# One attention and mixing kernel: x of batches 4 and 5 and the residual of batch 3 transposed by DMA instead of TensorE, in a new order of all steps

## The chip, the cores and the metric

The kernel runs on one core of a Trainium2 chip. The metric is device time in microseconds (us), the median of several executions. A NeuronCore has five engines that run side by side: TensorE (PE in the profile, with its weight loads as PEld), VectorE (DVE), ScalarE (ACT), GpSimd (POOL) and SyncE (SP), which here only issues DMA transfers. They wait for each other through semaphores. TensorE writes to PSUM, eight banks of 2 KB for each of 128 partitions; VectorE and ScalarE bring results from there to SBUF.

## The reference

```python
# attention: q, k, v are (8, 8, 576, 64)
q_d = q.reshape(B, H, Sd, 4, D).mean(axis=3)        # the same for k and v
out_up = np.repeat(sm_attn(q_d, k_d, v_d), 4, axis=2)
mask = np.abs(pos[:, None] - pos[None, :]) < 4
out_local = softmax(where(mask, scale * q @ k.T, -1e9)) @ v
x = (out_up + out_local).transpose(0, 2, 1, 3).reshape(B, S, H * D)   # (8, 576, 512)
# mixing
theta = x @ w_theta
zr, zi = x * cos(theta), x * sin(theta)
u = x + einsum('ts,bsd->btd', w_tok_r, zr) + einsum('ts,bsd->btd', w_tok_i, zi)
return u + np.maximum(u @ w_ch, 0.0)
```

Inputs and output are float32; the kernel works in bfloat16 inside and sums in float32.

## The kernel before

All eight batches go through the same chain of small steps, and several batches are under way at once. Each step has a two-letter name, and one step is one to a few dozen instructions of one engine:

- `lk`, `lq`, `lv`, `lw` load k, q and the two halves of v into one of 14 staging buffers (tile `st`), `ck`, `cq`, `cv` cast them. `tp` transposes k or q on TensorE (L304), `ev` brings the result to SBUF (L317). For batch 7 the DMA transposes them instead (`dk`, L308), from the cast to a staging buffer.
- The coarse attention takes means of four (`kd`, `qd`, L323 on VectorE or L331 with L334 and L337 on GpSimd), `sd`, `ed`, `nd`, `xn` (L427 to L459). The local attention is computed in windows of 64 positions: scores `ps` (L483, in 64*64 tiles), exponential `ex` (L491, ScalarE), product with a band mask `mk` (L502, VectorE or GpSimd), product with v `po` (L512), division `nm` (L520 and L521, VectorE).
- `xt` (L531) transposes the local output, `xa` (L537) adds the coarse one: the tile `xT` holds x with the channels on the partitions, in four column blocks of 128 channels.
- `th` (L548) multiplies x by w_theta, `cs` takes cosine and sine (L553, L554). z needs x with the positions on the partitions. `xm` (L587) transposes x on TensorE into PSUM, four 128x128 matmuls for 128 positions, and `zz` (L594, VectorE) multiplies it by cosine and sine. For the batches in `XDMA` there is no `xm`: `dx` (L590) has the DMA transpose one block of 128 channels for 512 positions from `xT` into the tile `xx`, four for a batch, and `zz` reads `xx`. The last 64 positions go their own way (`tt`, `ct`, `zt` L569, and `zp` on TensorE or `dz` L573 by DMA).
- `mx` (L610) is the mixing product over positions, nine matmuls for 288 columns; `ua` (L615) adds x and gives `uT`. `ch` (L635) multiplies by w_ch, and `rl` (L640) adds the residual and stores into `osb`. The residual is u with positions on the partitions, tile `ur`: for batches in `RPE` transposed on TensorE (`up`, L624) and copied (`uc`, L627), for the others by DMA (`du`, L619), four transfers for a batch. `st` (L644) stores.

There is one `xx`; of `xT`, `uT`, `ur` and `z` there are two each, taken in turn by batches. What engine runs a step, and into which bank pair or staging buffer, stands in the words of a long string `ORDER`; a word such as `x12` is a step's name and its place. Each engine runs its instructions in the order of that string, and nothing else sets it. Words with `wm` are matmuls on a constant tile that only keep TensorE active while it would wait (L715).

```python
XDMA = (6, 7)
RPE = (0, 1, 2, 3)
    def zz(b, c, w):
        x = xx[:, c, :] if b in XDMA else at.pop(("xm", b, c))
        nc.vector.tensor_tensor(out=z[b % 2][:, 2 * c:2 * c + 2, :],
                                in0=x.unsqueeze(1).to_broadcast([P, 2, DM]),
                                in1=cs[(4 * b + c) % NCS], op=ALU.mult)
```

Of the kernel before, what the change touches and what calls it, by code (L numbers as in the profile page):

```python
# [42 lines left out]

NSTG = 14

XDMA = (6, 7)

RPE = (0, 1, 2, 3)
ZPE = (0, 1, 2, 3)

QKD = (7,)
# [7 lines left out]
cqg lq7 lk8 lk9 tp45 cqg kcg kcg x12 lqa eva lqb kdg cvv kca cka wm62 tp67 lkc x13 lkd cvv eva ckv wm13 pv01 cqv lq0  # L59
la2 cqg lb1 tp45 qdv eva wm22 tp23 eva wm65 ps67 kdg vdv lq3 qdv ckg cka ps45 cag ex wm25 sd23 ex lb4 ed cbg lk5 sd01  # L60
cqg ps67 mkv ed po45 nm po23 nd45 nd01 la6 nm la7 xn xn lk8 mkg tp23 cag po45 ex xt6 po01 cqa eva la9 lqa mkg caa xd7
lqb ckg xca ckg nm tp23 nm xt4 xt5 lbd cag lbc cbg lb2 xt7 xa cqg lb1 eva lb0 cbg lb3 lb6 tp01 xa po23 th4 xa xm5 xa
lv7 cqg nm cbg th6 lw xt7 cbg th2 lv5 xm3 evv cbg ts cs tp01 lv8 lv9 cs cbg xa tt4 zz cs xm5 wp6 wp2 zz lw lw wp3 lw
lv4 lw cbg lqa zz ct lqd eva qdg ztv wp7 cba th4 wcv zp5 lkb xm6 wcv lkc kdg wcv wp2 wp3 wcv zcv wp0 wcv wp1 cs wp7
wca wcv ps45 lk2 lk1 wcv wcv ps23 te ex qdg ps01 lq0 zz kdv cva ex mx7 mx6 mx4 cvg ua sd23 cvg cvg mkv lc3 ex po01 ua
sd67 ed ed mkv mx5 ua nm po23 ua po01 cvg pv67 nm nm mkg vda mx4 ua po23 lq6 cqg po67 nd01 nm nd45 mx2 up3 xn lq7 ckg
xn cqg lk5 cka nm tp01 xd4 lk8 up5 uca eva xcv xt3 ucv lk9 tp67 cka xt4 xt0 ua ckg xt1 kdg lv4 xa xa xa mx5 xa eva lva
tp23 ua th4 xt0 lw xa evv cqg th5 xm1 lvb lcd lqc tt0 lw lk1 lv2 lv0 lw ts cs lw xm4 cqg cs tp67 ckg cqg th2 xm3 th5
ct lw cka zz tp01 cs qdg zz cs xm2 evv ztg lc6 lc5 zp4 mx6 ccg zz qdg zcv zz eva cvg mx7 ps45 te ex ua ps23 ua ckg kdv
ex mkv ps01 mx6 lq7 mx7 po45 sd23 ex lq8 lk3 kdg ed cvg sd01 cqg ckg ua lk4 lq9 mx6 tp23 mkv lva lw lvc lw nm ua tp45  # L70
up7 cvg mkv cvv ed mx0 eva cvg pv23 ccg ua ucv eva po67 po45 ua nm up1 nm vda ccg ccg ch0 nd67 lq1 xn nd23 lkb cqg cqa
tp45 uca qdg xn mx1 xd2 xt3 eva ps67 rl lq0 ua po45 xcv kdg qdg ps01 ch2 xa ckg ex mkg nm rl mx3 ps67 cqg lv2 cka po45
ex ua sd01 lkd xt2 ckg ex nm mx3 xt4 xt5 xa up2 ua cqa cqg tp67 cvv ed up3 xa evv uca th0 xa lv6 xt1 up2 xa lw th4 xm6
ucv ts cs uca th5 cvg lq5 ckg po01 cvg zz cs nm po23 xm7 cs ch6 nm tt4 tp01 lw ct tp23 th5 rl mkg ch4 lq7 zz st eva
evv rl po67 sd01 cs cqg cvg ztg po23 ch5 nm nm rl ch4 lv8 lw te ed cvg st pv67 vda zp0 zca lk4 cka lk3 lk1 tp23 cqa
mkg ckg lq9 lqb rl qdg lva lw xm1 eva ckg utg lv0 zz lw xm5 ch4 nd67 lvc zz xn lw nd01 mx5 lvd xn mx6 st ps23 rl lv2
ua po01 kdg nm ps45 ua mx7 lk5 ex xd0 cqa xt1 ex up6 ua xcv ucv lk6 kdv tp23 cqg utg mx0 tp45 qdg xa ua eva sd67 xt2
lv8 xt3 ch1 eva xa mkg ed xa th0 mkv rl cvg lk3 lw xt6 xt7 xa xa lw lk1 cvg th2 mx1 ua ts cs xm3 cvg tt0 zz th6 st lq4
cs cvg cka po45 dt cvg ckg ct po23 th7 mx1 ztg lk7 cs lvb nm pv45 cs ckg po67 cqg kdg lw nm ua sd23 mx0 cvg nm te ed
zp1 tp67 vdv zcv ht2 tp45 xm1 rt lw ua lq9 mx3 eva zz ps67 eva ua lva qdg po45 nm ex ps01 lq0 ex xm2 up3 zz lqc nd67  # L80
uca lvd tp45 cqa xm2 qdg xn nd01 zz mx3 cka cka xn mx2 xd0 up1 lk2 lv6 kdg st ua mx3 cqa mkv lw uca xcv eva tp67 xt0
up1 lk5 ua ua cva ucv xt4 xa mx5 st xa st eva ps23 mkg sd01 qdg po67 lw ed ua nm lv3 xt4 mx5 xt6 cva mx7 po01 ua ex
sd23 xa xa po45 lw nm cvg th6 nm lq4 cqv xt0 lw ed cvv xa ts cs tp23 mkv lv8 th1 cs xm4 ua ch5 kdg lw rl ch6 lv9 eva
tt0 th1 th7 xm5 pv23 utv ct ztg zz up0 ss cqg cs zz vdv mx1 uca ua xm0 lv1 lw st zz cs tp45 lv7 cvg lv0 cvg lqb nd23
# [17 lines left out]
def kernel(  # L102
# [53 lines left out]
    rl = tiles(2, [P, 2, 4], "rl", FP32)  # L156
# [509 lines left out]
    def span(*ns):  # L666
# [3 lines left out]
        return out  # L670

    STEPS = dict(
        k0=(lambda i, w: None, span(1)), kc=(kc, span(4)), la=(la, span(4)), ca=(ca, span(4)), lb=(lb, span(9)), cb=(cb, span(9)), lc=(lc, span(4)), cc=(cc, span(4)),
        wp=(wp, [(j,) for j in WPJ]), wc=(wc, [(j,) for j in WPJ]),
        lk=(load(0), span(B, 4)), lq=(load(1), span(B, 4)), ck=(cast(0), span(B, 4)), cq=(cast(1), span(B, 4)),
        tp=(tp, [x for x in span(B, 2, 2) if x[0] not in QKD]), dk=(dk, [x for x in span(B, 2, 2) if x[0] in QKD]), ev=(ev, span(B, 2, 2)),
# [48 lines left out]
    for kind in todo:  # L725
        assert next(todo[kind], None) is None, kind
    assert set(x[0] for x in at) <= {"v", "ot"}, at


# [28 lines left out]
```

## Time and profile before

| | |
|---|---|
| median of 3 runs | 230.73 us (230.29 to 231.62) |
| span of the profiled execution | 229.4 us; its own time was not taken apart from the runs, and the median lies 1.3 us above its span |
| PE busy | 219.7 us (96%), 3491 matmuls |
| DVE, ACT, POOL busy | 185.6, 159.3, 144.1 us |
| DMA queue of SP | 83.4% of 16 engines over the span |

The span runs from the first to the last instruction. Busy time counts the instructions of an engine; a busy PE may still be a PE that is filled with short or badly packed matmuls. Group rows read: line, engine, operation, written tile, read tiles, count, then busy us and mean ns of one. Rows of a timeline begin with start and length in us; a bracket at the end holds the idle time before and who ended it. Rows of a stretch hold its bounds and length, the busy time of PE, PEld, DVE, ACT and POOL with instruction counts, TensorE's granted clock, DMA share and GB/s. Rows of a tile give shortest, median and longest duration in ns.

### The profile page before, as it was taken

To read this page: it belongs to the slowest core of one execution; us is meant where nothing else is said; L and a number is where in the kernel's file an instruction comes from. 1 tells how busy PE (TensorE), PEld (TensorE's weight loads), DVE (VectorE), ACT (ScalarE), POOL (GpSimd) and SP (SyncE) were. 2 spreads that over 40 slices of the span, in tenths; PEclk is the share of its full clock that TensorE was granted. 3 is DMA by queue.
4 is the path that set the end of the run, shared out by engine and by line. 5 is a ranking of instruction groups with operands and counts; after the bars stand their busy time and mean duration, and the time that the engine had idled before them with its cause. 6 is when DMAs were issued, how large, how long until landed. Compare 5 with 4: busy or idle time off the path is not lost.

```text
span 229.4 us, 8506 instructions
## 1 busy us (share of the span) xinstructions
PE 219.7 (96%) x3491; PEld 154.2 (67%) x3491; DVE 185.6 (81%) x377; ACT 159.3 (69%) x239; POOL 144.1 (63%) x190
## 2 busy tenths in 40 slices
PE   7898899999999999999999999899999999999992
PEld 2455778696778765776788667676676665677740
DVE  5168999999899899797898969979898889476382
ACT  2389899759987899689887896779879258600000
POOL 7768999929999989991984456892697310200000
PEclk9999999999999999999999999999999999999998
DMA  6999999999989999999998007996576357376677
GB/s 181 387 391 391 268 190 222 374 271 226 235 270 249 248 345 177 231 261 233 291 220 211 21 17 191 302 214 126 136 132 187 68 118 206 74 207 160 94 239 241
DMA packets 76647, 49.35 MB, mean 215 GB/s; under 512 B 61120, under 2 KB 61120, under 8 KB 76608
## 3 DMA queue, kind: packets, MB, share of 16 engines
q1 hardware_dynamic: 76608, 48.81, 83.4%
q8 instruction: 27, 0.44, 0.8%
q14 instruction: 12, 0.10, 0.1%
HBM read 33.98 MB, written 9.44 MB: 189 GB/s over the span
## 4 chain that ended last, share of the span: by engine, by line
PE 86%; DVE 7%; DMA 3%; issue 2%; SPq 1%; ACT 0%; POOL 0%; DVEq 0%
PE PS L610 30%; PE PS L548 12%; PE PS L635 12%; PE PS L304 5%; PE PS L531 4%; PE PS L512 3%; DMA st<-in_v_dram 3%; PE PS L587 2%; PE PS L483 2%; PE PS L448 2%; PE PS L560 2%; DVE tmp L521 2%; PE PS L624 2%; PE PS L652 2%; PE PS L453 1%
## 5 line engine op out<-in xcount | busy, mean ns | idle before, releaser
L610 PE MATMUL PS<-WT,z 128*128 128x288 bf16 x576 | 77.9, 286 | 0.2 <-issue 0.2
L610 PEld LDWEIGHTS <-z 128*128 128x128 bf16 x576 | 54.3, 98 | 15.8 <-issue 0.9
L615 DVE TENSOR_TENSOR uT<-PS,xT 128x288 bf16<-128x288 f32 x64 | 28.8, 452 | 11.8 <-PE PS L610 10.9
L548 PE MATMUL PS<-wth,xT 128*128 128x512 bf16 x128 | 32.2, 379 | 0.0
L635 PE MATMUL PS<-wch,uT 128*128 128x512 bf16 x128 | 31.1, 379 | 0.0
L569 POOL TENSOR_TENSOR zT<-xT,cst 128x512 bf16<-128x512 bf16 x7 | 8.1, 1153 | 34.0 <-ACT cst L566 34.0
L521 DVE TENSOR_TENSOR tmp<-PS,rl 128x512 bf16<-128x512 f32 x40 | 27.7, 692 | 1.4
L502 POOL TENSOR_TENSOR pm<-pm,band 128x1024 bf16<-128x1024 bf16 (+1 forms) x14 | 25.0, 1789 | 4.5 <-ACT pm L491 4.5
L537 DVE TENSOR_TENSOR xT<-PS,xdT 128x464 bf16<-128x464 f32 (+1 forms) x40 | 24.0, 629 | 3.0 <-ACT xdT L471 2.0
L640 DVE SCALAR_TENSOR_TENSOR osb<-PS,ur 128x512 f32<-128x512 f32 x32 | 21.8, 685 | 4.7 <-PE PS L635 4.2
L491 ACT ACTIVATE pm<-PS 128x1024 bf16<-128x1024 f32 (+1 forms) x24 | 20.4, 879 | 6.5 <-PE PS L483 6.5
L553 ACT ACTIVATE cs<-PS,pihc 128x512 bf16<-128x512 f32 x32 | 22.2, 693 | 1.6 <-PE PS L548 1.4
L720 ACT ACT_TABLE_LOAD x15 | 19.2, 1283 | 0.3
L331 POOL TENSOR_TENSOR two<-kT 128x580 f32<-128x580 bf16 x13 | 15.0, 1152 | 7.0 <-ACT kT L317 5.3
L635 PEld LDWEIGHTS <-uT 128*128 128x128 bf16 x128 | 11.9, 98 | 11.1
L554 ACT ACTIVATE cs<-PS 128x512 bf16<-128x512 f32 x32 | 19.2, 601 | 0.0
L594 DVE TENSOR_TENSOR z<-PS,cs 128x1024 bf16<-128x1024 bf16 x24 | 16.0, 682 | 2.3 <-PE PS L587 1.8
L548 PEld LDWEIGHTS <-xT 128*128 128x128 bf16 x128 | 11.3, 98 | 9.6 <-DVE xT L537 0.2
L331 POOL TENSOR_TENSOR two<-qT 128x576 f32<-128x576 bf16 x13 | 14.9, 1145 | 4.3 <-ACT qT L317 4.0
L438 ACT ACTIVATE pd<-PS 128x864 bf16<-128x864 f32 x16 | 13.8, 888 | 5.0 <-PE PS L427 4.9
L397 POOL CAST v_w<-st 128x512 bf16<-128x512 f32 x26 | 16.8, 672 | 0.0
L317 ACT COPY qT<-PS 128x1152 bf16<-128x1152 bf16 x13 | 14.6, 1121 | 2.0 <-PE PS L304 2.0
(116 smaller groups left out, 427.0 us busy)
## 6 DMA issues: line engine op xcount, KB each, us to landing
st<-in_k_dram SPq DMA_DIRECT2D x32, 288.0 KB, 6.0
st<-in_q_dram SPq DMA_DIRECT2D x32, 288.0 KB, 6.1
st<-in_v_dram SPq DMA_DIRECT2D x70, 128.0 KB, 5.2
out_dram<-osb SPq DMA_DIRECT2D x32, 256.0 KB, 2.4
st<-in_v_dram SPq DMA_DIRECT2D x4, 288.0 KB, 3.2
st<-in_moe_w_tok_r_dram SPq DMA_DIRECT2D x4, 288.0 KB, 6.5
st<-in_moe_w_tok_i_dram SPq DMA_DIRECT2D x4, 288.0 KB, 7.4
st<-in_moe_w_theta_dram SPq DMA_DIRECT2D x4, 256.0 KB, 6.3
```

The costliest lines, as they stand in the source:

```text
L331: nc.gpsimd.tensor_tensor(out=t, in0=src[:, :, 0:2], in1=src[:, :, 2:4], op=ALU.add)
L491: nc.scalar.activation(out=pm[(3 * b + u) % NPM][:, :, 0:n].rearrange("p e c j w -> p e (c j w)"), in_=at.pop(("ps", b, u))[:, :, 0:4 * W ...
L502: EW[w].tensor_tensor(out=t, in0=t, in1=m, op=ALU.mult)
L521: nc.vector.tensor_tensor(out=tmp[(NCH * b + c) % NTMP].rearrange("p g (j d) -> p g j d", d=D), in0=ps[:, :, :, 0:D], in1=r.unsqueeze(3).t ...
L537: nc.vector.tensor_tensor(out=xT[b % 2][:, :, CH * c:CH * c + cnt].rearrange("p e (m j) -> p e m j", j=4), in0=at.pop(("xt", b, c))[:, :, ...
L548: nc.tensor.matmul(out=ps, lhsT=xT[b % 2][:, dc, P * c:P * c + P], rhs=wth[:, dc, :], start=(dc == 0), stop=(dc == 3))
L553: nc.scalar.activation(out=t[:, 0, :], in_=ps, func=AF.Sin, bias=pihc, scale=1.0)
L554: nc.scalar.activation(out=t[:, 1, :], in_=ps, func=AF.Sin, bias=0.0, scale=1.0)
L610: nc.tensor.matmul(out=ps, lhsT=z[b % 2][:, j, P * dc:P * dc + P], rhs=WT[:, j, cols], start=(j == 0), stop=(j == 8))
L615: nc.vector.tensor_tensor(out=uT[b % 2][:, dc, cols], in0=at.pop(("mx", b, i)), in1=xT[b % 2][:, dc, cols], op=ALU.add)
L635: nc.tensor.matmul(out=ps, lhsT=uT[b % 2][:, dc, P * c:P * c + P], rhs=wch[:, dc, :], start=(dc == 0), stop=(dc == 3))
L640: nc.vector.scalar_tensor_tensor(out=o, in0=at.pop(("ch", b, c)), scalar=0.0, in1=ur[b % 2][:, c, :], op0=ALU.max, op1=ALU.add)
```

## The change

Two lists of batches change, so that x of batches 4 and 5 and the residual of batch 3 go through `dx` and `du` instead of `xm` and `up`. `ORDER` is replaced as a whole. The batches' steps need no longer come in rising order: a word now carries the step's indices (`tp011.01` is batch 0, pair 1, q, into banks 0 and 1). Line numbers after L46 move by 32: L590 becomes L622, L610 L642, and so on.

```diff
-XDMA = (6, 7)
-
-RPE = (0, 1, 2, 3)
+XDMA = (4, 5, 6, 7)
+
+RPE = (0, 1, 2)
...
 ORDER = """
-l10 l11 c1g c1g k0 l12 lk3 l14 ckg c1v lk5 wm0b t101 c1g e1a kcg wm24 t123 e1a lq6 wm45 x12 cva ckg x13 cva x10 cvv
...
+l103.0 lq02.1 cq02.a lq03.2 c103.a cq03.v l100.3 c100.g l101.4 wm.28 tp011.01 ev011.v qd01.v l102.5 c101.g wm.24
...
-    todo = {kind: iter(seq) for kind, (_, seq) in STEPS.items()}
+    todo = {(kind,) + tuple(args) for kind, (_, seq) in STEPS.items() for args in seq}
     for word in ORDER.split():
-        kind, place = word[:2], word[2:]
+        word, _, place = word.partition(".")
+        kind, args = word[:2], tuple(int(x) for x in word[2:])
...
-        STEPS[kind][0](*next(todo[kind]), place)
+        todo.remove((kind,) + args)
+        STEPS[kind][0](*args, place)
```

The order moves on every engine. Two places, before and now:

SyncE's queue where batch 5's x is under way. Before, it holds the transposes of batch 7's k and q (L308), of batch 4's residual (L619), of a tail (L647) and of batch 5's rest of z (L573), loads of v (L349) and stores (L644):

```order
L308 DMA_TRANSPOSE st_135<-k_tm_76 128x9x128
L644 DMA out_dram<-osb_121 128x512
L308 DMA_TRANSPOSE st_138<-q_tm_79 128x9x128
L647 DMA_TRANSPOSE utr<-ut_117 128x4x128
L619 DMA_TRANSPOSE ur_114<-uT_112 128x4x128
L349 DMA st_132<-in_v_dram 64x8x64
L619 DMA_TRANSPOSE ur_114<-uT_112 128x4x128
L308 DMA_TRANSPOSE st_129<-k_tm_74 128x9x128
L349 DMA st_128<-in_v_dram 64x8x64
L308 DMA_TRANSPOSE st_136<-q_tm_77 128x9x128
L573 DMA_TRANSPOSE z_104<-zT 128x4x128
```

Now, with x of batch 5 (L622), k and q of batch 7 (L340), loads of q (L320), a store (L676) and the rest of z (L605):

```order
L622 DMA_TRANSPOSE xx<-xT_102 128x4x128
L320 DMA st_132<-in_q_dram 128x576
L622 DMA_TRANSPOSE xx<-xT_102 128x4x128 x2
L340 DMA_TRANSPOSE st_133<-k_tm_74 128x9x128
L676 DMA out_dram<-osb_123 128x512
L320 DMA st_134<-in_q_dram 128x576
L340 DMA_TRANSPOSE st_140<-k_tm_76 128x9x128
L605 DMA_TRANSPOSE z_104<-zT 128x4x128
L622 DMA_TRANSPOSE xx<-xT_102 128x4x128
```

The four transfers of x come in, two transposes and the rest of z stand between the third and the fourth of them, and the residual of batch 4 is later in the queue.

VectorE where batch 4's z is made. Before, z (L594) takes x from PSUM (PS) and cosine and sine from `cs`; with copies for the coarse attention (L413, L416), L615 and L640 in between:

```order
L594 TENSOR_TENSOR z0_103<-PS_61,cs0_105 128x1024
L594 TENSOR_TENSOR z0_103<-PS_61,cs1_106 128x1024
L413 CAST vd1_73<-PS_61 128x8x64
L416 CAST vd1_73<-PS_61 32x4x64 x2
L615 TENSOR_TENSOR uT1_113<-PS_61,xT1_102 128x288
L594 TENSOR_TENSOR z0_103<-PS_61,cs2_107 128x1024
L640 SCALAR_TENSOR_TENSOR osb0_119<-PS_61,ur0_114 128x512
```

Now (L626 is z, L647 was L615, L552 and L553 were L520 and L521, L672 was L640):

```order
L626 TENSOR_TENSOR z0_103<-xx_110,cs1_106 128x1024
L647 TENSOR_TENSOR uT1_113<-PS_61,xT1_102 128x288
L552 RECIPROCAL rl0_93<-PS_61 128x8
L553 TENSOR_TENSOR tmp1_88<-PS_61,rl0_93 128x512
L626 TENSOR_TENSOR z0_103<-xx_110,cs0_105 128x1024
L672 SCALAR_TENSOR_TENSOR osb2_121<-PS_61,ur0_114 128x512
L626 TENSOR_TENSOR z0_103<-xx_110,cs2_107 128x1024
L626 TENSOR_TENSOR z0_103<-xx_110,cs3_108 128x1024
```

z reads `xx`, which is in SBUF, and its four instructions stand in the order 1, 0, 2, 3 of positions.

More of the change, by code (lines that the diff above doesn't have):

```diff
@@ L63 @@
[L63 to L72, printed above, removed]
@@ L98 @@
+ch72.7 rl72.v ch71.1 rl71.v st72 st71
 """
@@ L722 @@
             continue
-        STEPS[kind][0](*next(todo[kind]), place)
+        todo.remove((kind,) + args)
+        STEPS[kind][0](*args, place)
         pin()
-    for kind in todo:
-        assert next(todo[kind], None) is None, kind
+    assert not todo, todo
     assert set(x[0] for x in at) <= {"v", "ot"}, at
```

101 lines of the change are left out of this document (71 added, 30 removed).

## The prediction

> **What bounds the kernel now.** I read the page first: shares of the engines, then the chain that ended last.
>
> ```profile
> span 229.4 us, 8506 instructions
> PE 219.7 (96%) x3491; PEld 154.2 (67%) x3491; DVE 185.6 (81%) x377; ACT 159.3 (69%) x239; POOL 144.1 (63%) x190
> PE 86%; DVE 7%; DMA 3%; issue 2%; SPq 1%; ACT 0%; POOL 0%; DVEq 0%
> ```
>
> TensorE (PE) is busy for 96% and carries 86% of the chain. A busy PE is not a PE at its peak, so next come the stretches: busy time after 28.8 us, when the first product of x and w_theta (L548) starts.
>
> ```profile
> 28.80:160.00 131.20, 130.03 (x2346) 95.82 (x2343) 116.42 (x230) 110.90 (x168) 102.29 (x124) 1.00 0.93 223
> 125.00:160.00 35.00, 34.06 (x571) 23.84 (x562) 29.14 (x61) 28.22 (x42) 22.52 (x25) 1.00 0.68 146
> ```
>
> PE is busy 130.03 of 131.20 us to 160 us, so 1.17 us are lost there. VectorE (DVE) is second with 116.42 us, which is 89%. DMA is 0.68 busy between 125 and 160 us. So the time is the sum of PE's steps, each at its start-to-start distance, plus a start that PE spends waiting and a tail. PE's timeline gives the distances.
>
> ```profile
> 102.58 1.03 PE L548 MATMUL PS<-wth,xT 128*128 128x512 bf16 x4
> 103.45 0.57 PE L531 MATMUL PS<-ident,tmp 128*128 128x116 bf16 x8
> ...
> 106.51 1.03 PE L548 MATMUL PS<-wth,xT 128*128 128x512 bf16 x4
> 107.47 0.45 PE L512 MATMUL PS<-v_w,pm 64*64 64x65 bf16 x32
> ...
> 114.01 0.39 PE L587 MATMUL PS<-ident,xT 128*128 128x128 bf16 x4
> 114.23 1.02 PE L610 MATMUL PS<-WT,z 128*128 128x288 bf16 x7
> ```
>
> The first column is a step's start. Four transposes of x (L587) take 114.23 - 114.01 = 0.22 us; four of a residual (L624) are the same instruction on the same shape. A product of four L548 takes 0.87 us when a full-array step follows (102.58 to 103.45) and 0.96 us when one in 64*64 tiles does (106.51 to 107.47): going over to small tiles costs 0.09 us.
>
> **The change part by part.** *Transposes that leave PE.* x of batches 4 and 5 is 8 steps, the residual of batch 3 is 4: 12 x 0.22 = 2.6 us, all on the path, since PE has no idle time that could swallow it. The eight x steps lose no VectorE work: the product z (L594) is made either way, and costs the same (below). The four residual copies (L627) go from ScalarE and VectorE, off the path.
>
> *Tile shapes.* Counted step by step in the two orders, changes of the array's tile shape rise from 101 to 109. But those between full rows and 128*72 cost nothing in the trace; those into or out of 64*64, 128*32 and 128*64 are 76 before and 70 after. 6 x 0.09 = 0.5 us gained. In the count of all changes, the new order does not do what its words say. The bank pairs were neighbours before too, except that one score step now takes banks 3 and 4: nothing.
>
> *What the transfers cost.* Twelve DMA transposes come on the SyncE queue. The rows of the tile xx show what such a one costs for batches 6 and 7.
>
> ```profile
> L590 SPq DMA_TRANSPOSE xx<-xT x8: 1189/1264/2213, 179.1 to 199.6; - x8
> L594 DVE TENSOR_TENSOR z<-xx,cs x8: 682/682/692, 191.7 to 206.5; 128x1024 bf16<-128x1024 bf16 x8
> DMA to landing us min/median/max: 2.4/2.5/3.3
> L308 SPq DMA_TRANSPOSE st<-k_tm x2: 1318/1819/2320, 147.0 to 158.1; - x2
> ```
>
> Each holds the queue for 1.26 us and lands 2.5 us after its issue; a transpose of k (last row) holds it for 1.8 us in the median of two. Twelve hold the queue for 15 us in a stretch where DMA is 0.68 busy, so the transfers as such fit. What counts is the latency. Every product z reads all four column blocks of xx, so in batch 5 it waits for the last L622 in the listing of SyncE's queue above, which now stands behind two k or q transposes and the rest of z. Queue time from the first L622 to the last: four x and the rest of z at 1.26, two L340 at 1.8, three plain transfers at about 0.5: 6.3 + 3.6 + 1.5 = 11.4 us, landing 2.5, four z of 0.68 and a pair of other VectorE instructions of 0.9 between them: 17.5 us. PE's steps between the last piece of x and the first mixing step (L642 now, L610 before) that needs z add up to 17.5 us by their distances in the trace (seven mixing steps of 1.1, seven products of 0.87, the small ones). There is no margin. For batch 4 the like sum is 14.5 us against 14.7 us.
>
> *VectorE reading twice from SBUF.* The z of batches 4 and 5 now takes both its inputs, xx and cs, from SBUF, where before one came from PSUM (the listings of VectorE above). That such instructions wait for GpSimd (POOL) is seen where the mask product (L502, also two SBUF inputs) meets one:
>
> ```profile
> 40.33 0.72 DVE L502 TENSOR_TENSOR pm<-pm,band 128x1024 bf16<-128x1024 bf16 x1
> ...
> 144.05 2.12 POOL L502 TENSOR_TENSOR pm<-pm,band 128x1024 bf16<-128x1024 bf16 x1 [2.60 <-ACT pm L491]
> 144.73 1.73 DVE L502 TENSOR_TENSOR pm<-pm,band 128x512 bf16<-128x512 bf16 x1
> ...
> 147.36 0.32 PE L512 MATMUL PS<-v_w,pm 64*64 64x65 bf16 x16 [0.94 <-DVE tmp L521]
> ```
>
> With 1024 columns it takes 0.72 us beside short POOL casts. With half the columns, at 144.73, it takes 1.73 us: it ends 0.29 us after POOL's own mask product, which ended at 146.17. PE then waits 0.94 us for the instruction behind it, L521 (last row): most of the 1.17 us lost to 160 us. The z rows quoted above, 682 to 692 ns, were taken while POOL was idle. In 125 to 160 us POOL is busy 22.52 of 35 us, 64%. A z that comes at any moment waits the rest of a POOL instruction: between 0 and 1.45 us (146.17 - 144.73). Weighting POOL's pieces there (0.6, 1.2 and 2.1 us) by their length, the mean rest is about 0.6 us; with the 64% it is 0.35 us for each z, 1.4 us for the four of a batch. Bounds: 0 and 4 x 1.45 = 5.8 us. As there is no margin, this goes to PE. I take 1.0 us for a batch, 2.0 in all, since some of the planned instructions in between can give way.
>
> [...]
>
> *The new order elsewhere.* The three half-width mask products leave VectorE for POOL, and with them the wait at 146 us: 0.9 us gained. VectorE also takes over casts of v (4 to 15 from staging), two evictions of k or q, one of v, and gives up the copies of vd.
>
> ```profile
> L397 DVE CAST v_w<-st 128x512 bf16<-128x512 f32 x4 | 2.5, 623 | 0.0
> L317 DVE COPY kT<-PS 128x1152 bf16<-128x1152 bf16 x4 | 5.4, 1347 | 0.0
> L323 DVE TENSOR_REDUCE kd<-kT 128x290 bf16<-128x1160 bf16 x3 | 4.1, 1352 | 0.0
> L413 DVE CAST vd<-PS 128x512 bf16<-128x512 f32 x3 | 2.0, 679 | 0.0
> L416 DVE CAST vd<-PS 32x256 bf16<-32x256 f32 x6 | 2.5, 412 | 0.0
> ```
>
> 11 x 0.62 + 3 x 1.35 - 3 x (0.68 + 2 x 0.41) = +6.4 us; smaller moves cancel but for a few tenths. So VectorE would be busy some 122 us of the 128 us that PE then needs where it was 116 of 131. For waits that come of that I add 0.5 us; the bounds are 0 and eight waits, one for each batch, of the 0.94 us seen above: 7.5 us. I stay near 0 because 30 us with VectorE at 96% pass without one, as the row under rival B shows.
>
> *The start.* Warming matmuls fall from 37 to 18.
>
> ```profile
> 1.26 2.74 PE L227 MATMUL PS<-warm 128*128 128x512 bf16 x6 [1.26 <-DVE warm L198]
> ...
> 28.79 1.04 PE L548 MATMUL PS<-wth,xT 128*128 128x512 bf16 x4
> ```
>
> They fill waits. The first L548 product waits for VectorE's queue. In the new order this has, from the third load (5.9 us) to the first piece of x, two copies (L317) and three reductions (L323) of 1.35 us and about 12.5 us of shorter ones: 25 us, and with 2 to 4 us of waits for loads 27 to 29 us, as now. Since one transpose step (0.5) and one small product (0.2) now lie ahead of that point, up to 0.7 us is gained; I take 0.4. It could lose 2.1 us: the first warming matmuls run at 2.74 us for six, twice the 0.22 us that L548 shows, for about 4.2 us, and if the array fell back to that pace once more half of such a stretch is lost. The tail (eight products, last store) stays.
>
> Sum: -2.6 - 0.5 - 0.9 + 2.0 + 0.5 - 0.4 = -1.9 us, a span of 227.5 us. The profiled execution's span lies 1.3 us under the median of 230.73 us, so 228.8 us.
>
> **The rivals.** *A: z waits for POOL in full.* Place: the four z of batch 4 and of batch 5. If POOL always has a next instruction ready, it gets in between each two z, and each z waits a whole one, 1.1 us by the mean of the pieces and 1.45 by the row: 4 to 6 us a batch. From about 2 us a batch the gain is gone. At 5: 230.7 - 4.0 + 10 - 3 (what PE can still take from steps in between) = 233.7 us, slower. For it: no margin, POOL 64% busy. Against: in the new order other VectorE instructions stand between the z, and POOL waits too.
>
> *B: VectorE becomes the bound.* 122 us of work in 128 us leaves no room for its waits on transfers; each 1% that it loses is 1.3 us. With 2% lost: 228.8 + 2.6 - 0.5 (the allowance that it replaces) = 230.9 us, no gain. Against: the trace has VectorE at 29.84 of 31.2 us for a stretch without PE waiting:
>
> ```profile
> 28.80:60.00 31.20, 31.20 (x541) 24.11 (x538) 29.84 (x59) 27.52 (x45) 26.32 (x35) 1.00 1.02 249
> ```
>
> *C: a cold start.* With half the warming gone, first steps at half pace: 228.8 + 2.1 + 0.4 = 231.3 us, no change.
>
> *D: the gains come and no new wait does*: 230.7 - 4.0 - 0.7 (the start's gain) = 226.0 us.
>
> **How the numbers follow.** The runs shown spread by 0.6%, so about 0.5% (1.15 us) is what can be told from no change: faster is below 229.6, slower above 231.9. Chances: forecast 0.42 (own range 227.3 to 230.0), D 0.10, A 0.20, B 0.20, C 0.08. Faster: 0.85 of the forecast, all of D, a fifth of B: 0.36 + 0.10 + 0.04 = 0.50. Slower: 0.85 of A, 0.55 of B, 0.4 of C: 0.17 + 0.11 + 0.03, with rounding 0.32. The rest, 0.18, is no change. The likeliest is 228.8 us. The range runs from 226.3 (into D) to 234.0 us (A at 5 us a batch, and a little over it).
>
> **What would show it.** In the changed profile: PE's busy time without the warming falls by 3 us; L619 (transposes of x now) has 64 and L656 48 instructions; z from xx (L626) takes 0.7 us in the rows of batches 6 and 7 and up to 2 us between 125 and 170 us; PE's idle time before the first L642 of batches 4 and 5 is 1 us each; no PE wait near 146 us on L553. It is wrong if PE idles over 3 us after 29 us, or if the first L580 product starts after 30 us.

## The result: 4% slower, and the profile after

The changed kernel takes 242.7 us (median of 4 runs, 238.8 to 245.5) where the kernel before, beside it on the same chip, takes 230.6 us (230.3 to 231.6). The ratio is 1.040, 95% interval 1.030 to 1.050; it leaves runs out that lie far above the fastest of their kernel, and so is below that of the medians. The forecast of 228.8 us had the wrong sign, and the range to 234.0 us does not hold the time. The profiled execution took 243.1 us with a span of 241.3 us. The two longest stalls that are read from it below stand in other profiles too: the early one of 2.2 us in those of x_before_rest_of_z and batch7_copies_on_scalar, the one of 2.0 us in batch 5 in those of st00_dt0_later and wch_cast_on_scalar.

The page of the changed kernel: span, busy times, the digit rows of TensorE and of its clock in 40 slices, and the chain by engine.

```profile
span 241.3 us, 8321 instructions
PE 216.6 (90%) x3401; PEld 151.4 (63%) x3424; DVE 195.2 (81%) x385; ACT 157.5 (65%) x239; POOL 138.8 (58%) x179
...
PE   7877989999969988999999998898699899999992
...
PEclk9999999999999999999999999999979999999997
...
PE 23%; DVE 12%; DMA 11%; SPq 8%; issue 5%; POOL 4%; ACT 1%; DVEq 0%; POOLq 0%
```

PE is busy 3.1 us less than before, but not in the way that was forecast: its warming matmuls fall from 12.7 to 8.6 us of busy time, and the rest goes from 208.4 to 208.9 us, where the forecast was 3 us less without the warming. (A few of PE's records are missing, and the lost clock shown below adds to its busy time.) The span is 11.9 us longer. The chain could be followed back only to 84 us, so its shares add up to 64% of the span. PE carries 23 of these 64, a good third, where before it carried 86 of 99; VectorE, DMA, SyncE's queue (SPq) and POOL carry most of the others. The digit 7 in slice 30 of the clock's row is new too. Stretches of the kernel before (stretch, its length, then busy us of PE, PEld, DVE, ACT and POOL with their instructions, clock, DMA share, GB/s):

```profile
30.00:60.00 30.00, 30.00 (x530) 23.40 (x528) 28.67 (x56) 26.33 (x43) 25.12 (x33) 1.00 1.02 247
60.00:100.00 40.00, 39.76 (x812) 29.11 (x811) 35.78 (x70) 33.64 (x51) 37.50 (x47) 1.00 1.00 255
100.00:140.00 40.00, 40.00 (x647) 29.13 (x645) 34.01 (x70) 34.63 (x52) 24.72 (x31) 1.00 0.75 172
140.00:180.00 40.00, 39.06 (x721) 27.88 (x720) 34.54 (x69) 31.35 (x46) 29.48 (x28) 1.00 0.80 177
```

The same stretches of the changed kernel:

```profile
30.00:60.00 30.00, 28.98 (x556) 22.61 (x557) 26.63 (x55) 25.33 (x44) 24.32 (x28) 1.00 0.94 259
60.00:100.00 40.00, 35.93 (x628) 26.09 (x630) 36.33 (x69) 29.32 (x44) 33.20 (x40) 1.00 0.84 193
100.00:140.00 40.00, 38.81 (x745) 28.53 (x748) 35.73 (x71) 35.17 (x54) 27.99 (x31) 1.00 1.02 223
140.00:180.00 40.00, 34.28 (x476) 23.08 (x479) 30.72 (x59) 27.02 (x39) 19.82 (x22) 0.96 0.86 179
```

Before, PE idles 1.2 us in these 150 us. Now it idles 1.0, 4.1, 1.2 and 5.7 us, 12.0 in all (missing records included). Of that, 5.1 us lie ahead of 100 us. The first of the twelve new transfers, one of batch 3's residual, is issued at 129.9 us, the first of x at 134.8 us (rows of xx, below). So a good part of the loss cannot come from them.

The longest stall of the early half is at 67.6 us. PE's timeline there:

```profile
65.83 1.76 PE L642 MATMUL PS<-WT,z 128*128 128x288 bf16 x13
69.81 0.45 PE L544 MATMUL PS<-v_w,pm 64*64 64x65 bf16 x32 [2.23 <-DVE v_w L429]
```

VectorE's:

```profile
65.08 2.63 DVE L534 TENSOR_TENSOR pm<-pm,band 128x1024 bf16<-128x1024 bf16 x2
67.64 1.37 DVE L276 CAST wch<-st 128x512 bf16<-128x512 f32 x1
68.93 0.83 DVE L429 CAST v_w<-st 128x512 bf16<-128x512 f32 x1
```

PE waits 2.23 us for a cast of v (L429). The cast's data landed by 55.8 us, but in VectorE's order it stands behind two mask products (L534) and a cast of w_ch (L276) that takes 1.37 us. The groups on VectorE show a move that the prediction priced only as busy time (L429 is L397 of its rows, where the count was four):

```profile
L429 DVE CAST v_w<-st 128x512 bf16<-128x512 f32 x15 | 10.4, 707 | 1.2 <-DMA st<-in_v_dram 1.2
L626 DVE TENSOR_TENSOR z<-xx,cs 128x1024 bf16<-128x1024 bf16 x16 | 12.8, 824 | 5.5 <-ACT cs L586 2.8 <-DMA xx<-xT 2.2 <-issue 0.5
L626 DVE TENSOR_TENSOR z<-PS,cs 128x1024 bf16<-128x1024 bf16 x16 | 10.5, 681 | 1.0 <-ACT cs L586 1.0
```

Fifteen casts of v stand there for four. While GpSimd is idle such a cast takes 0.42 us, beside GpSimd up to 1.50. z from `xx` takes 824 ns in the mean, z from PSUM 681 in the same execution.

The second place is batch 5's z. Rows of the tile `xx` (shortest, median, longest in ns):

```profile
L622 SPq DMA_TRANSPOSE xx<-xT x16: 1188/1260/2216, 134.8 to 211.9; - x16
L626 DVE TENSOR_TENSOR z<-xx,cs x16: 680/684/1957, 144.8 to 217.9; 128x1024 bf16<-128x1024 bf16 x16
```

The chain that ended last, there (start, length):

```profile
166.95 1.72 DMA xx<-xT
168.67 2.68 issue
171.44 1.29 DVE z L626 x2
...
173.49 3.52 DVE z L626 x2
```

POOL's timeline in the same stretch:

```profile
172.75 2.15 POOL L346 COPY qT<-st 128x1152 bf16<-128x1152 bf16 x1 [4.57 <-DMA st<-q_tm]
```

PE's:

```profile
170.41 1.27 PE L642 MATMUL PS<-WT,z 128*128 128x288 bf16 x9
173.63 0.42 PE L499 MATMUL PS<-ident,xdn 72*128 72x72 bf16 x8 [1.96 <-DVE tmp L553]
173.88 1.85 PE L667 MATMUL PS<-wch,uT 128*128 128x512 bf16 x4
...
177.06 1.16 PE L642 MATMUL PS<-WT,z 128*128 128x288 bf16 x7 [0.46 <-DVE z L626]
```

The last x of batch 5 is issued at 166.95 us and lands at 171.3. VectorE has stood there for 2.8 us with everything behind it. Two z at 0.69 us follow, then two that take 3.5 us together (1.96 the longest), while POOL copies q of batch 7 (172.75 to 174.90) and then sums it. PE waits 1.96 us for the division of the local attention (L553) behind the first two z, and 0.46 us for z itself. And in the row of 173.88 a product of four L667 takes 1.85 us where L548 (now L580), of the same shape, took 1.03 in the prediction's rows. The granted clock is 0.51 there; the last section has its rows.

### The profile page after: what moved, and what is told of

The parts are those of the page before. It is cut to its first block, busy times and chain, and to the rows that moved or that the text cites. A ratio compares the mean times of both kernels' runs of the same rounds, so it can differ in the third digit from the quotient of the medians.

```text
span 241.3 us, 8321 instructions
## 1 busy us (share of the span) xinstructions
PE 216.6 (90%) x3401; PEld 151.4 (63%) x3424; DVE 195.2 (81%) x385; ACT 157.5 (65%) x239; POOL 138.8 (58%) x179
## 4 chain that ended last, share of the span: by engine, by line
PE 23%; DVE 12%; DMA 11%; SPq 8%; issue 5%; POOL 4%; ACT 1%; DVEq 0%; POOLq 0%
PE PS L642 10%; DMA st<-in_v_dram 5%; PE PS L667 5%; DVE z L626 4%; DMA xx<-xT 4%; SPq L622 4%; SPq L381 3%; PE PS L580 3%; POOL two L363 2%; DVE osb L672 2%; DMA st<-in_k_dram 1%; DVE v_w L429 1%; PE PS L563 1%; PE PS L336 1%; DVE tmp L553 1%
## 5 line engine op out<-in xcount | busy, mean ns | idle before, releaser
L642 PE MATMUL PS<-WT,z 128*128 128x288 bf16 x576 | 78.8, 287 | 1.0 <-DVE uT L647 0.5
L642 PEld LDWEIGHTS <-z 128*128 128x128 bf16 x576 | 54.4, 98 | 16.6 <-DVE z L626 1.0
L647 DVE TENSOR_TENSOR uT<-PS,xT 128x288 bf16<-128x288 f32 x64 | 27.9, 450 | 11.2 <-PE PS L642 9.6
L667 PE MATMUL PS<-wch,uT 128*128 128x512 bf16 x120 | 32.0, 387 | 1.4 <-DVE uT L647 0.9
L580 PE MATMUL PS<-wth,xT 128*128 128x512 bf16 x114 | 30.1, 379 | 1.8 <-DVE xdT L503 0.6
L672 DVE SCALAR_TENSOR_TENSOR osb<-PS,ur 128x512 f32<-128x512 f32 x32 | 21.8, 686 | 9.7 <-PE PS L667 6.1
L553 DVE TENSOR_TENSOR tmp<-PS,rl 128x512 bf16<-128x512 f32 x40 | 27.7, 692 | 1.4
L534 POOL TENSOR_TENSOR pm<-pm,band 128x512 bf16<-128x512 bf16 (+1 forms) x14 | 22.9, 1638 | 8.2 <-ACT pm L523 8.2
L601 POOL TENSOR_TENSOR zT<-xT,cst 128x512 bf16<-128x512 bf16 x6 | 7.1, 1188 | 23.9 <-ACT cst L598 23.9
L667 PEld LDWEIGHTS <-uT 128*128 128x128 bf16 x128 | 11.9, 99 | 11.6 <-issue 1.4
L329 POOL CAST q_tm<-st 128x576 bf16<-128x576 f32 x21 | 14.8, 715 | 7.2 <-DMA st<-in_q_dram 6.0
L363 POOL TENSOR_TENSOR two<-qT 128x576 f32<-128x576 bf16 x14 | 16.6, 1185 | 3.6 <-ACT qT L349 2.4
L429 POOL CAST v_w<-st 128x512 bf16<-128x512 f32 x18 | 12.2, 686 | 11.1 <-DMA st<-in_v_dram 11.0
L580 PEld LDWEIGHTS <-xT 128*128 128x128 bf16 x128 | 11.4, 98 | 10.7 <-issue 0.8
L329 POOL CAST k_tm<-st 128x576 bf16<-128x576 f32 x20 | 14.4, 741 | 6.3 <-DMA st<-in_k_dram 6.3
L626 DVE TENSOR_TENSOR z<-xx,cs 128x1024 bf16<-128x1024 bf16 x16 | 12.8, 824 | 5.5 <-ACT cs L586 2.8
```

Of the source, the lines that this page charges most:

```text
L329: COPY[w](out=to[:, r, :], in_=of[:, r, :])
L363: nc.gpsimd.tensor_tensor(out=t, in0=src[:, :, 0:2], in1=src[:, :, 2:4], op=ALU.add)
L534: EW[w].tensor_tensor(out=t, in0=t, in1=m, op=ALU.mult)
L553: nc.vector.tensor_tensor(out=tmp[(NCH * b + c) % NTMP].rearrange("p g (j d) -> p g j d", d=D), in0=ps[:, :, :, 0:D], in1=r.unsqueeze(3).t ...
L580: nc.tensor.matmul(out=ps, lhsT=xT[b % 2][:, dc, P * c:P * c + P], rhs=wth[:, dc, :], start=(dc == 0), stop=(dc == 3))
L642: nc.tensor.matmul(out=ps, lhsT=z[b % 2][:, j, P * dc:P * dc + P], rhs=WT[:, j, cols], start=(j == 0), stop=(j == 8))
```

## The experiments

All times are medians of 4 runs, each beside the kernel before on the same chip (230.6 to 231.4 us). Ratios are to that kernel and are made as the one above; where they and the medians differ, the text goes by the ratios.

| run | us (lowest to highest) | ratio, 95% interval |
|---|---|---|
| changed kernel | 242.7 (238.8 to 245.5) | 1.040 (1.030 to 1.050) |
| old_order_new_assign | 250.4 (249.4 to 252.3) | 1.085 (1.078 to 1.091) |
| new_assign_old_order | 251.0 (250.5 to 252.6) | 1.087 (1.083 to 1.091) |
| old_assign_new_order | 249.8 (247.7 to 254.3) | 1.078 (1.069 to 1.086) |
| no_x_transfers_45 | 237.9 (236.0 to 241.3) | 1.026 (1.021 to 1.032) |
| no_twelve_transfers | 240.3 (238.9 to 241.9) | 1.040 (1.033 to 1.046) |
| x45_on_scalar_queue | 258.4 (257.5 to 259.6) | 1.118 (1.114 to 1.122) |
| late_stores_on_scalar | 247.7 (246.3 to 250.2) | 1.070 (1.063 to 1.076) |
| two_queue_waits_later | 249.3 (247.8 to 252.0) | 1.077 (1.069 to 1.084) |
| st00_dt0_later | 244.8 (244.0 to 246.7) | 1.060 (1.055 to 1.066) |
| half_of_v_loads | 241.4 (240.2 to 242.9) | 1.046 (1.039 to 1.052) |
| x_before_rest_of_z | 242.0 (241.0 to 243.2) | 1.047 (1.042 to 1.053) |
| batch7_copies_on_scalar | 243.3 (242.1 to 244.2) | 1.053 (1.047 to 1.058) |
| wch_cast_on_scalar | 243.0 (242.9 to 246.2) | 1.056 (1.048 to 1.064) |
| v_casts_on_scalar | 244.2 (244.0 to 244.5) | 1.056 (1.053 to 1.059) |
| filled_stalls | 244.6 (242.9 to 249.2) | 1.055 (1.048 to 1.062) |
| no_twelve_less_vector | 237.8 (236.6 to 238.2) | 1.027 (1.023 to 1.032) |
| mended_order | 237.4 (236.5 to 238.8) | 1.029 (1.023 to 1.035) |
| mended_no_twelve | 239.2 (238.4 to 240.4) | 1.034 (1.027 to 1.041) |

### Is it the assignment or the order?

**old_assign_new_order.** After's order; the twelve transfers become TensorE steps again, put in where a bank was free:

```diff
-XDMA = (4, 5, 6, 7)
-RPE = (0, 1, 2)
+XDMA = (6, 7)
+RPE = (0, 1, 2, 3)
-... dx41 ... dx40 ... dx43 ... dx42 zz41.v ... zz40.v ...
+... xm41.6 ... xm40.3 ... xm42.4 ... zz41.v ... xm43.3 ...
```

> The new order kept, but x of batches 4 and 5 and the residual of batch 3 go back to TensorE (12 transposing transfers fewer, 48 transposes and 4 copies more on TensorE and ScalarE). Theory Transfers (SyncE's queue is full: 12 transfers at 1.24 us of issue each delay the loads and x behind them): the time falls back to 231 to 234 us, since only the order's other changes are left. Theory Order (the new order asks for v and x later than their users can bear, whoever transposes): it stays at 239 to 243 us. A split: TensorE stood still 5.1 us between 30 and 140 us in the changed kernel against 0.3 before, and no x of batch 4 was transposed before 134.8 us, so if both hold, about 236 to 238 us.

249.8 us, beyond either theory. PE stands at the new L619 steps, 0.5 to 1.3 us each between 144 and 180 us, where they wait for the last reader of their bank: the banks that were free in the order had been read only just before. (One residual step of batch 3 also came behind the step that overwrites its source.) So this run says nothing on the transfers. Its stalls of 2.2, 0.7 and 0.5 us at 68, 89 and 92 us are those of the changed kernel: they belong to the order.

**new_assign_old_order** and **old_order_new_assign.** Before's order, with `dx` behind the additions that fill its source and `du` behind `ua`, in place of `xm`, `up` and `uc`; the second has `dx` behind all five additions, as it must:

```diff
-... ua31 ... xa44 ... xm40 ... zz40 ... xm41 ... zz41 ... up30 ... uc30 ...
+... ua31 du30 ... xa44 dx40 dx41 dx42 dx43 ... zz40 ... zz41 ...
```

> The order of before kept, with the 12 transposing transfers put in right behind the last addition that they need, in place of the TensorE steps. Theory Transfers: 12 x 1.24 us more on SyncE's queue come back as waits, 236 us or more. Theory Order: the old order hides them, 2.6 us of TensorE are saved, 228 to 232 us.

> The order of before, with the twelve transposing transfers in place of the TensorE steps; each transfer of x stands behind all five additions that fill its source (in new_assign_old_order it stood ahead of the last, which then waited for it 5 to 6 us). Theory Transfers (each costs 1.24 us of SyncE's queue, and what stands behind comes late): 15 us more in a queue that waited 12.0 us in one place near 124 to 136 us; 234 to 245 us. Theory Order (the assignment is harmless, the new order does the harm): 228 to 232 us.

251.0 and 250.4 us. Waits of SyncE's queue in the second (total, times, longest):

```profile
SPq L645 <- DVE uT L641: 15.7, 5, 10.7
```

Its rows of `xx` (z is L620 there; the second row is VectorE's idle time ahead of z):

```profile
L620 DVE TENSOR_TENSOR z<-xx,cs x16: 676/682/1336, 139.4 to 224.6; 128x1024 bf16<-128x1024 bf16 x16
...
  DMA xx<-xT: 12.4, 3
```

The first residual transfer waits 10.7 us in the queue for its source, with the loads behind it, and VectorE stands 12.4 us in three places for x that is still on its way. The Transfers theory holds for an order that was made without them: twelve transfers in these places, for 2.6 us of PE's steps, cost 20 us. Other places were not tried, and it does not yet say what they cost in the new order.

**no_x_transfers_45** and **no_twelve_transfers.** After's order without the transfers:

```diff
     def dx(b, dc, w):
+        if b in (4, 5):
+            return
     def zz(b, c, w):
-        x = xx[:, c, :] if b in XDMA else ...
+        x = wth[:, c, :] if b in (4, 5) else xx[:, c, :] if b in XDMA else ...
     def du(b, dc, w):          # only in no_twelve_transfers
+        if b == 3:
+            return
```

> The changed kernel without the eight transfers of x of batches 4 and 5; z of these batches multiplies w_theta's blocks, which are in SBUF as x would be, so VectorE reads the same way. Theory Transfers: 8 x 1.24 us of SyncE's queue and the waits for xx at 145, 171 and 176 us go, 233 us or less. Theory Order: only the direct waits for xx go (0.96 + 0.90 + 2.02 + 0.78 us at most), 238 to 240 us. Rival of VectorE's reads: z still beside GpSimd, so its slow instructions (up to 1.96 us) stay.

> The changed kernel without any of the twelve new transfers (x of batches 4 and 5 and the residual of batch 3 left out; z of 4 and 5 reads w_theta's blocks, the residual what was there). TensorE's steps are gone too, so this is the new order alone with 2.6 us less of TensorE. Theory Transfers: 229 us or less. Theory Order: the stalls at 67, 75, 90 and 93 us stay (4 to 5 us) and the slow z beside GpSimd (2 to 4 us): 234 to 237 us.

237.9 and 240.3 us, ratios of 1.026 and 1.040: against 1.040 of the changed kernel the first is faster, though the intervals just overlap, and the second is the same. Both are 6 to 9 us slower than before, although PE has its 2.6 us less to do. So most of the loss is in the order and in what z now reads. The 5.1 us that PE idles ahead of 100 us are the order's alone, since the first z from `xx` starts at 144.8 us; how the rest divides was not measured. The rows of z in no_twelve_transfers:

```profile
L628 DVE TENSOR_TENSOR z<-wth,cs x8: 680/1120/1792, 143.7 to 172.7; 128x1024 bf16<-128x1024 bf16 x8
```

z of batches 4 and 5, with x in place at once, takes 1.12 us in the median and up to 1.79. In batch 5 it now runs beside POOL's copies and sums of batch 7, which begin at 165.1 us here and at 172.8 us in the changed kernel. At 169 and 174 us PE waits 1.9 and 0.8 us behind it, much as it did behind x.

### Is SyncE's queue the limit?

It issues for 8.4 to 9.5 of every 10 us between 130 and 180 us, so five runs take load or waits off it.

**x45_on_scalar_queue.** `(nc.scalar if b in (4, 5) else nc.sync).dma_start_transpose(...)` in `dx`.

> The changed kernel with the eight transfers of x of batches 4 and 5 issued from ScalarE instead of SyncE; the DMA engines move the same. If SyncE's issue time is the limit (it issues for 8.4 to 9.5 of every 10 us between 130 and 180 us), 9.9 us of it go to ScalarE, which has 27 us busy of 40 there: 237 to 240 us. If the DMA engines are the limit, or the transfers' landing, no gain: 241 to 245 us.

258.4 us. ScalarE's order is held by the transfers that it issues, up to 2.3 us each; at 183 us PE stands 6.8 us.

**late_stores_on_scalar.** `(nc.scalar if b > 2 else nc.sync).dma_start(...)` in `st`.

> The changed kernel with the stores of batches 3 to 7 issued by ScalarE instead of SyncE: 20 x 0.53 us of issue leave SyncE after 175 us, where it issues 7 to 9.4 of every 10 us; ScalarE is busy there 18 of 61 us. Theory Queue: 2 to 5 us less, 238 to 241 us. If ScalarE's order is tight (x45_on_scalar_queue cost 16 us), it waits for VectorE's results ahead of cosine and sine: 243 to 250 us.

247.7 us. A store on ScalarE waits for VectorE, and the cosine behind it comes late: PE stands 2.5 us at 200 us for that. Both runs failed by the same side effect, so they leave the question open.

**two_queue_waits_later** and **st00_dt0_later.** Words moved in the order:

```diff
-lq51.4 st00 cv34.g ... st01 ... lk60.5 ... lv40.7 lw40 dt0 ... lv54.4 ... lw54
+lq51.4 cv34.g ... st01 ... lk60.5 st00 ... lv40.7 lw40 ... lv54.4 ... lw54 dt0
```

> The changed kernel with three of SyncE's 211 transfers later: the stores st00 and st01 behind the next loads of k and v, and the transpose of the tails dt0 fourteen transfers later. In the changed kernel SyncE stood 3.8 us at st00 and 5.1 us at dt0 with loads behind them. Theory Queue (a transfer that waits holds all loads behind it, and the queue never catches up again, since it is full from 93 to 172 us): 236 to 239 us, with the stalls of TensorE at 88, 92, 145 and 159 us shorter. Theory VectorE (casts and z beside GpSimd are what is late): under 1 us gained, 241 to 243 us.

> The changed kernel with two of SyncE's transfers later: the first store st00 three loads later (its buffer is needed soon after, which two_queue_waits_later had overlooked for st01), the transpose of the tails dt0 behind 18 more loads and stores. SyncE stood 3.8 us at st00 and 5.1 us at dt0. Theory Queue (what SyncE loses in waits at 80 to 93 us it never gets back, since it is full from then on, and late loads and late x stop TensorE): 3 to 6 us less, 237 to 240 us. Theory Order of VectorE (its own order is what is late): under 1 us, 242 to 243 us.

In the first, which had both stores behind `lw40` instead, SyncE waited 15.3 us at st00, because the next writer of the buffer now came ahead of the store (two stored blocks hold the next values): 249.3 us. The second, as shown, gives 244.8 us: not faster. The waits of 3.8 and 5.0 us at these words are gone, loads go out 5 us earlier at 93 us, but the queue then waits 2.7, 4.5 and 2.9 us at later words for data that is not there, and the first x goes out at 135.2 us (134.8 before).

**half_of_v_loads.** `if b > 3: return` in `lw`: 20 loads less.

> The changed kernel without the second half of v's loads for batches 4 to 7 (20 of SyncE's 211 transfers, 0.65 us of issue and 64 KB each; the casts read what was in the buffer). No other engine's work changes. Theory Queue (SyncE's queue paces the kernel from 93 us on, so that what is mended elsewhere is given back): 13 us less in the queue, x, v and batch 7's k and q earlier: 234 to 239 us. Theory VectorE (its own order and slow instructions): 241 to 243 us.

241.4 us, a ratio of 1.046: no gain with 13 us of issue gone. For the new order theory Queue falls, as far as the time to issue goes.

### Is it VectorE's order and its slow instructions?

**x_before_rest_of_z**: `dz4` behind `dx42`, `dz5` behind `dx52`.

> The changed kernel with the transfers of the rest of z (dz4, dz5) behind the last transfers of x instead of ahead of them. VectorE waited for the last x of batch 4 until 144.6 us and of batch 5 until 171.3 us, and TensorE for VectorE 0.9 and 2.0 us. If x in the queue is what VectorE waits for there: 2 to 3 us less, 239 to 241 us. If z is late anyway, by z's slow instructions beside GpSimd: no change, 242 to 244 us.

242.0 us, 1.047: no gain. The stalls at 167, 171 and 176 us are gone and all z takes under 0.78 us. PE waits more at 156 and 160 us (1.0 and 1.1 us for k's means and v, 0.8 and 0.5 us in the changed kernel), and anew at 184 (1.0) and 233 us (2.0).

**batch7_copies_on_scalar**: `ev701.g`, `ev710.g` become `.a`.

> The changed kernel with two copies of k and q of batch 7 (2.15 and 2.18 us on GpSimd, 172.8 to 179.7 us) on ScalarE. Two z of batch 5 ran beside them and took 3.5 us for 1.4. [...] Theory Queue: under 0.5 us of change, since z also waited for x until 171.3 us.

243.3 us: no gain. All z takes 0.69 us at most, but the copies end later on ScalarE, and PE waits 2.4 us at 182 us for them.

**wch_cast_on_scalar**: `cc3.v` becomes `cc3.a`, `cv21.v` moves ahead of `mk21.v`.

> The changed kernel with one cast of w_ch (1.37 us on VectorE at 67.6 us, SyncE waited 3.1 us for its buffer) on ScalarE, and the cast of v that TensorE waited for at 67.6 us ahead of two products with the mask (2.7 us on VectorE). The stall of 2.3 us at 67.6 us goes in both theories. Theory Order (each stall of TensorE adds up): 2 to 4 us less, 239 to 241 us. Theory Queue (SyncE paces the rest): what TensorE gains it gives back by 100 us, and only the 3 us that SyncE gains may count.

243.0 us. The stall at 67 us shrinks from 2.2 to 1.5 us and no more, since the product also needs the masks. Nothing is gained at the end.

**v_casts_on_scalar**: fifteen `cv` words from `.v` to `.a`.

> The changed kernel with fifteen casts of v (L429, batches 1 to 7) on ScalarE instead of VectorE; the new order had moved twelve more of them to VectorE than before (19 for 7, with those of batch 0). They took 0.42 us alone and up to 1.50 us beside GpSimd, 10.6 us in all, in front of z and of what TensorE waits for. Theory VectorE (these casts, slow beside GpSimd, are what delays TensorE): the stalls at 67, 88, 92 and 189 us go, 3 to 6 us less, 237 to 240 us. Theory Other (the order is tight in every queue, so what goes in one place comes back in another): within 1.5 us of 242.7, or slower through ScalarE's queue.

244.2 us. PE's idle time between 60 and 100 us falls from 4.1 to 2.0 us, and new stalls come at 133 us (ScalarE's queue) and grow at 175 us.

**no_twelve_less_vector**: no_twelve_transfers with the edits of the last run and of batch7_copies_on_scalar.

> no_twelve_transfers (240.3 us) with the fifteen casts of v and two copies of k and q of batch 7 on ScalarE, so that nothing slow stands beside batch 5's z: there z took 1.15 to 1.79 us instead of 0.69, a cast 1.50, and TensorE stood still 1.9 and 1.1 us. Theory two chains (x by transfer, and VectorE beside GpSimd, end at about the same time, so that taking away one alone brought 0.7 to 2.4 us): with both gone 232 to 235 us. Theory Other: 238 to 241 us.

237.8 us, 1.027 for 1.040 of no_twelve_transfers: 3 us, where at least 5 were expected. z is fast (0.69 us in the median), and now PE waits 2.4 us at 175 us for four copies of batch 7 in a row on ScalarE, with 3.4 us at half clock behind it (the mean granted clock of this execution is 0.993).

**filled_stalls**: `wm.28` ahead of `po21`, `wm.58` ahead of `xd5`.

> The changed kernel with eight idle matmuls (1.7 us) in front of each of the two longest stalls of TensorE, at 67 and 171 us. After the stall of 2.0 us at 171 us the granted clock was half for 3.4 us (1.7 us lost); in runs of other kernels also after the one at 67 us. Theory Clock (a pause of about 2 us costs 1.7 to 3.4 us of clock on top): no drop to half between 30 and 235 us, 1.5 to 3.5 us less, 239 to 241 us. Otherwise the matmuls only add to the queue: 242.5 to 245 us.

244.6 us (up to 249.2): no gain, though the clock stays full between 20 and 240 us (9 in these slices of its page; mean granted clock 0.997). PE waits for z 0.95 and 1.14 us at 175 us, where the changed kernel had 0.46 us: there the time came back as waits for data.

**mended_order.** Several mends at once; everything is computed:

```diff
-cc3.v  cv33.v cv30.v cv32.v cv71.v
+cc3.a  cv33.a cv30.a cv32.a cv71.a
-ua13.v mk21.v ... mk20.v ... cc3.v ... cv21.v
+ua13.v cv21.v mk21.v ... mk20.v ... cc3.a
-dz4 dx43 mx34.3 dx42        ... dz5 cv71.v cq73.g dx52
+dx43 mx34.3 dx42 dz4        ... cv71.a cq73.g dx52 dz5
```

> The changed kernel, complete, with the mends that apply to one place each put in together: one cast of w_ch and four of v on ScalarE, a cast of v ahead of two mask products, the last x of batches 4 and 5 ahead of the rest of z. Theory two chains (each mend alone only uncovers the other): 237 to 240 us. Theory Queue: 240 to 243 us, as with each alone.

237.4 us, 1.029 (1.023 to 1.035). Parts of it alone had 1.047 (1.042 to 1.053, x_before_rest_of_z) and 1.056 (1.048 to 1.064, wch_cast_on_scalar), and fifteen casts of v on ScalarE, of which four are used here, had 1.056: together they gain 4 us or more over each. The four casts were not run without the rest. Against the changed kernel itself the gain is 5 us by the medians and under 3 us by the ratios, whose intervals overlap a little; the slowest run is as fast as its fastest. The stretches:

```profile
60.00:100.00 40.00, 37.29 (x697) 27.14 (x686) 34.98 (x68) 31.89 (x51) 34.12 (x41) 1.00 0.85 211
...
140.00:180.00 40.00, 37.40 (x581) 26.13 (x584) 33.04 (x66) 29.55 (x42) 20.20 (x22) 1.00 0.94 186
```

And z, from its rows of `xx`:

```profile
L626 DVE TENSOR_TENSOR z<-xx,cs x16: 679/684/835, 141.5 to 212.4; 128x1024 bf16<-128x1024 bf16 x16
```

PE idles 2.7 us for 4.1 and 2.6 us for 5.7, z takes 0.84 us at most, and the mean granted clock is 1.000.

**mended_no_twelve**: mended_order with the edits of no_twelve_transfers.

> mended_order (237.4 us) without the twelve transfers (as in no_twelve_transfers: x of batches 4 and 5 and the residual of batch 3 left out). What remains between the two is what the transfers cost where the order has been mended for them. If they cost by lateness still: 232 to 235 us. If the mends have covered them: 236 to 238 us, and then all that lies between this time and before's, plus the 3 us that TensorE was spared, is the new order's own.

239.2 us, not faster than with the transfers: the intervals of the two ratios overlap. So in a mended order the twelve transfers cost nothing that can be measured. Why not less, the row of z shows:

```profile
L628 DVE TENSOR_TENSOR z<-wth,cs x8: 681/1360/2430, 141.3 to 170.8; 128x1024 bf16<-128x1024 bf16 x8
```

Without the wait for x, z falls under POOL's copies and sums of batch 7: 1.36 us in the median, up to 2.43, 5.4 us above eight at 0.68. Two late chains end at about the same time here, x by transfer and z beside POOL. Taking one away uncovers the other.

## Why the prediction was wrong

**The step that failed is "The new order elsewhere": +0.5 us, bounds 0 and 7.5.** Gaps between PE's instructions after 30 us (missing records left out) add up to about 13 us in the changed kernel and 1.2 before. Of the 13 us, 3.3 are at z of batches 4 and 5 (145, 171 and 176 us). The rest, 9 to 10 us, is what this term should have held. It lies in a dozen places of 0.3 to 2.2 us, and most ends with an instruction of VectorE. That this instruction stood behind others in VectorE's order was looked at in the longest one (2.2 us at 67 us); at the others only the instruction that PE waited for is known. VectorE was hardly fuller: between 60 and 100 us it is busy 36.3 of 40 us, and 35.8 before. The reason given for staying near 0, that VectorE was 96% busy for 30 us without a wait, was no reason: that was an order in which nothing late was needed soon. Counting 11 more casts of v at 0.62 us each missed that one could take up to 1.50 us and stand ahead of what PE waits for. (VectorE's busy time rose by 9.6 us, where 6.4 were summed.) The bound of one wait a batch at 0.94 us was too low in number and in size.

**Steps that leave PE, -2.6 us:** right. L619 has 64 and L656 48 instructions. Counted from each instruction's start to the next one's, these transposes take 6.7 us, and 9.2 us before. The sign that was named for it, 3 us less of PE's busy time without the warming, did not come (208.9 us for 208.4): 1.7 us of lost clock (3.4 us at 0.51) are in it, and where the rest comes from was not found.

**Transfers.** Each holds the queue for 1.26 us, as said. From the first x of batch 5 to the last the queue took 11.6 us (156.6 to 168.2) where 11.4 were counted. The last landing took 4.3 us after its issue, not 2.5, and the four z with what lies between them 5.6 us, not 3.6. From the first issue to the end of the last z it took 20.4 us where 17.5 were counted. So the chain that had "no margin" was 3 us late. For batch 4 it took 14.3 us, 14.5 counted. The mechanism was named; the price was not drawn from it. Landings of up to 5.0 us, as now, were not in the row of before, which ended at 3.3.

**z beside POOL, +2.0 us:** the size came out (16 z of `xx` took 2.3 us more than at 0.68), but by luck: nearly all of it is in two z of batch 5, none in batch 4, where 1.0 us for each batch was taken. As a cost it shared its place with x's lateness. Alone it is worth more: 5.4 us of slow z in mended_no_twelve, most of it in batch 5. z from PSUM stays at 0.67 to 0.69 us in the same execution, though 15 of these 16 run beside a POOL instruction. Rival A was thus real in batch 5 (z of 1.96 and 1.63 us), but not the main loss.

**The wait at 146 us, -0.9 us:** gone on L553, and one of 0.9 us stands at 145 us, for x of batch 4.

**The start, -0.4 us:** the first L580 starts at 27.35 us, 1.4 us earlier. Rival C did not come. **Rival B** had the right engine and the wrong mechanism: VectorE is busy 81%, as before.

**What stays open.** The mended order is still 6.5 us slower than before, with PE about 8 us in gaps after 30 us, and what those come from was not looked into. No run here beats the kernel before, so whether some order lets the new assignment gain is not known. Tile shapes (-0.5 us) were not separated; the traces hold 82 changes into or out of small tiles before and 80 after, so at 0.09 us each they are worth 0.2 us at most.

## What to carry to other kernels

Where every engine runs a fixed order, a busy share says what an engine could do, not when each result comes: for every instruction that moves, find what PE will need next from that queue and what stands ahead of it. Price a moved instruction at its slowest row beside the other engines, not its mean. And if a mend brings nothing, do not take the place for harmless: where several chains end together, mending one may only uncover the next, as in mended_no_twelve.

## What the runs showed of the hardware

**After a stall of 1.96 us TensorE's granted clock was 0.51 for 3.4 us; after one of 2.23 us in the same execution it stayed at 1.00.** Stretches of the changed kernel, two at the second place above and one at the early stall:

```profile
170.50:173.90 3.40, 1.44 (x19) 1.06 (x18) 2.43 (x5) 1.49 (x3) 1.15 (x1) 1.00 1.18 193
173.90:177.30 3.40, 2.94 (x17) 1.22 (x14) 3.40 (x3) 3.21 (x4) 3.24 (x3) 0.51 0.76 233
68.10:71.50 3.40, 1.69 (x48) 1.50 (x49) 3.20 (x7) 0.59 (x1) 3.40 (x6) 1.00 0.53 119
```

Stretches of no_twelve_transfers around the same early stall:

```profile
66.10:69.50 3.40, 1.19 (x10) 0.71 (x8) 3.40 (x5) 1.19 (x2) 3.40 (x4) 1.00 0.56 91
69.50:72.90 3.40, 3.38 (x49) 2.68 (x50) 2.40 (x6) 1.12 (x1) 3.32 (x6) 0.50 0.81 232
```

The stall of 1.96 us ends at 173.63 us, and from 173.90 us on the clock is 0.51. The stall of 2.23 us ends at 69.81 us, and the clock is 1.00 from 20 to 173.9 us. In no_twelve_transfers the clock is 0.50 from 69.5 us, behind a stretch in which PE is busy 1.19 of 3.40 us. Why one of the two stalls of the changed kernel was followed by half clock and the other was not is not shown. Half clock for 3.4 us costs PE up to 1.7 us of work (3.4 x 0.5, an estimate from these rows). The longest pause of the kernel before after 28.8 us is 0.94 us, and its clock is 1.00 from 20 to 227 us; old_order_new_assign has a mean granted clock of 0.963. Runs of the changed kernel spread by 2.8%, those of the kernel before by 0.6%, and the clock explains little of that: the mean granted clocks of the four runs (0.988 to 0.993) account for 1.2 us between them at most, where their times lie 6.7 us apart.

**A cast of v, with one input from SBUF, took 0.42 us alone and up to 1.50 us beside GpSimd.** The longest cast of v in the changed kernel ends 0.28 us after the mask product on POOL that it met:

```profile
86.73 2.12 POOL L534 TENSOR_TENSOR pm<-pm,band 128x1024 bf16<-128x1024 bf16 x1
87.63 1.50 DVE L429 CAST v_w<-st 128x512 bf16<-128x512 f32 x1
```

The four casts of v on VectorE that met no POOL instruction took 0.42 to 0.43 us there, ten of the eleven others 0.56 to 1.50 us.
